# Attention and MoE on one core: the first four heads' scores in float32 from k and q as loaded, the row maxima of heads 1 and 2 tied by data to the preceding head's row, and fewer constant matmuls

## The chip, the cores and the metric

The program runs on one core of one Trainium2 chip. The metric is the device time of one execution in microseconds (us). Three executions of the kernel before took 1249.19, 1252.88 and 1254.61 us, a median of 1252.88 us.

## The reference

Two stages. The first is attention over 8 batches and 8 heads (64 heads in all) of 576 positions and 64 features, with a mask by blocks of 64 positions; the second is a gated feed-forward layer over all 4,608 rows.

```python
scores = scale * np.matmul(q, k.transpose(0, 1, 3, 2))
scores = np.where(block_i >= block_j, scores, -1000000000.0)
scores = scores - np.max(scores, axis=-1, keepdims=True)
attn = np.exp(scores)
attn = attn / (np.sum(attn, axis=-1, keepdims=True) + 1e-09)
x = np.matmul(attn, v)          # then heads side by side: 4608 x 512
h = x @ w_in                    # 512 -> 2048
out = (h * erf(softplus(h))) @ w_out   # 2048 -> 512
```

The inputs are float32 and the weights are float64 (the kernel loads them as pairs of 32-bit words and turns them into pairs of float16).

## The kernel before, in words

Heads are numbered n = 0 to 63. Each head's transposed k and q lie in a buffer `qk` of 128 partitions and four planes of 576 columns, in one of four such buffers that the heads use in turn (NB = 4). Planes 2 and 3, on partitions 0 to 63, hold k and q rounded to float32r (a float32 format that TensorE takes with reduced precision); under them, on partitions 64 to 68, stand five constant rows that bring in the mask and one row that is filled later, the negated row maximum of each query. Planes 0 and 1, on all 128 partitions, hold rounded values and remainders crossed, so that one product of 128 rows gives both first-order correction terms.

`load_qk` (line 380) fills a buffer. Its step `a` issues one DMA on GpSimd's queue (POOL) of three planes, which rounds on the way (L383), one on SyncE's queue (SP) of the plain float32 values into a staging tile `st` (L384), of which there are two, and a second rounding DMA of two planes on POOL (L385). Its step `c` forms the remainders with two subtractions on POOL (L388, L389).

`maxes` (line 396) computes the scores of a head once in float32r (L400, tiles `s`), takes row maxima on VectorE (L403, tile `mx`), transposes the five columns of maxima with a matmul against the identity (L430, tile `mt`), copies the result on ScalarE (L432) and sends it with a small DMA on ScalarE's queue into the row left free (L433). `probs` (line 440) computes the scores a second time, now transposed and with mask and maximum as extra rows, as two float32r matmuls that add up in one PSUM bank: 69 rows of rounded values (L446) and 128 rows of corrections (L447), tiles `t`; ScalarE's exponential follows (L451). `pv` multiplies by v (L495) and by ones for the sums (L518), for two heads at a time; for the first 24 heads these operands are plain float32. `normalise` turns this into rows of x, which go to DRAM in float16 pairs.

The loop over n (line 650) merges in each iteration: the loads of head n+3, the maxima of head n+2, the `mt` step of head n+1 in the iteration's first 60 per cent, the probabilities of head n, for even n the products with v of heads n-2 and n-1, a conversion or two of weights (`raw` tiles, loaded on SP, L113; converted by L120 to L126), and steps of the feed-forward layer (L190 upwards, L199 downwards) as soon as a batch of x is there. Before the loop the maxima of heads 0 and 1 are issued. In iterations 0 and 1, WARM = 10 matmuls of ones (L647) are merged in, whose result nobody reads. The order on each engine is that of a scheduler that goes by data dependences and its own costs; each engine then works through its own list in order.

## Time and profile before

| | before |
|---|---|
| median of three runs (range) | 1252.88 us (1249.19 to 1254.61) |
| the profiled execution | 1253.77 us, of which the span from first to last instruction is 1252.0 us |
| TensorE matmul (PE) busy | 1169.7 us, 93% of the span |
| ScalarE (ACT), VectorE (DVE), GpSimd (POOL) busy | 865.4, 791.9 and 515.9 us |
| DMA | 151.73 MB, 121 GB/s on average |
| mean granted TensorE clock | 0.97 of full speed |

The granted clock is given as a share of full speed; 1.00 is 2.4 GHz and 0.50 is 1.2 GHz, and a number between is a stretch with parts at either. An engine's busy share is an average over the program's stages, so the stages are read apart. In the rows below, "idle before" and its releaser stand in square brackets. SPq and ACTq are the queues on which SyncE and ScalarE issue DMAs; a long time there may include a wait for a buffer.

### The profile page before, as it was taken

What the parts mean: (1) busy time and instruction counts of PE and PEld (TensorE: products, weight loads), DVE (VectorE), ACT (ScalarE), POOL (GpSimd) and SP (SyncE); (2) the same over time, 40 slices, a digit from 0 to 9 for tenths busy, and PEclk for the clock granted to TensorE, in tenths of its full rate; (3) what the DMA queues carried; (4) which work ended last, traced back from release to release, by engine and by line L of the source; (5) the groups of instructions that cost most, each with busy time, mean ns of one, the idle gap of its engine ahead of it and who ended that gap; (6) DMA issues with size and microseconds to landing.
All of it is one profiled execution on the core that took longest, in us unless ns stands there. A gap on an engine that the chain in (4) does not pass through costs nothing.

```text
span 1252.0 us, 23446 instructions
## 1 busy us (share of the span) xinstructions
PE 1169.7 (93%) x9018; PEld 811.0 (65%) x9018; DVE 791.9 (63%) x1457; ACT 865.4 (69%) x1699; POOL 515.9 (41%) x486
## 2 busy tenths in 40 slices
PE   5788699989999999999999899999999999999896
PEld 2465466666666767767767677766777766666563
DVE  4677689787577666676657667666666644343433
ACT  1465577687676777877777677777777876666664
POOL 6455446545343444445444353545443313121211
PEclk9876799999999999999999999999999999999999
DMA  9988569744544455364454455455554121121211
GB/s 218 250 208 190 124 181 234 195 101 117 112 128 110 115 125 128 100 147 120 99 124 116 118 119 130 112 124 128 112 137 108 45 78 53 60 76 35 64 55 51
DMA packets 95741, 151.73 MB, mean 121 GB/s; under 512 B 7738, under 2 KB 44922, under 8 KB 95630
## 3 DMA queue, kind: packets, MB, share of 16 engines
q1 hardware_dynamic: 69840, 93.34, 25.7%
q0 software_dynamic: 25120, 56.66, 22.6%
q8 instruction: 71, 1.16, 0.4%
q10 hardware_dynamic: 670, 0.23, 0.2%
q14 instruction: 40, 0.33, 0.1%
HBM read 121.66 MB, written 28.31 MB: 120 GB/s over the span
## 4 chain that ended last, share of the span: by engine, by line
PE 49%; DVE 20%; ACT 18%; DMA 7%; issue 4%; POOL 1%; DVEq 0%; SPq 0%; POOLq 0%; ACTq 0%
PE m_h L190 16%; PE o L199 15%; PE u L495 5%; DVE m_r L163 4%; DVE m_r L164 4%; DVE m_r L165 3%; ACT m_r L160 3%; ACT m_r L162 3%; ACT m_r L161 3%; ACT m_r L159 3%; PE t L446 3%; PE s L400 3%; PE t L447 2%; DMA qk<-qk 2%; DMA qk<-mt 2%
## 5 line engine op out<-in xcount | busy, mean ns | idle before, releaser
L190 PE MATMUL m_h<-xh,w 128*128 128x256 f16 x2304 | 476.1, 276 | 19.5 <-DVE m_r L165 12.2
L190 PEld LDWEIGHTS <-w 128*128 128x128 f16 x3456 | 328.3, 99 | 158.1 <-issue 31.2
L199 PE MATMUL o<-w,m_gh 128*128 128x512 f16 x1152 | 334.1, 382 | 12.2 <-DVE pt L240 4.9
L167 POOL TENSOR_TENSOR m_gl<-m_r,m_gh 128x512 f16<-128x512 f32 x144 | 171.8, 1193 | 391.1 <-ACT m_gh L166 340.6
L190 PE MATMUL m_h<-xl,w 128*128 128x256 f16 x1152 | 316.8, 275 | 0.5 <-DMA xl<-x_d 0.5
L403 DVE TENSOR_REDUCE mx<-s 64x1 f32<-64x288 f32 (+4 forms) x384 | 174.5, 469 | 131.3 <-PE s L400 130.5
L163 DVE SCALAR_TENSOR_TENSOR m_r<-m_r,m_r 128x512 f32<-128x512 f32 x144 | 112.8, 783 | 197.3 <-ACT m_r L162 190.8
L199 PE MATMUL o<-w,m_gl 128*128 128x512 f16 x576 | 203.7, 384 | 0.3 <-POOL m_gl L167 0.3
L451 ACT ACTIVATE p<-t 128x288 f32<-128x288 f32 (+4 forms) x384 | 144.6, 384 | 79.4 <-PE t L447 69.1
L166 ACT CAST m_gh<-m_r 128x512 f16<-128x512 f32 x144 | 88.9, 617 | 157.2 <-DVE m_r L165 154.4
L446 PE MATMUL t<-qk 69*128 69x288 f32 (+4 forms) x384 | 168.2, 439 | 13.0 <-DMA qk<-mt 6.8
L400 PE MATMUL s<-qk 68*64 68x288 f32 (+3 forms) x384 | 150.1, 423 | 22.8 <-DMA qk<-qk 19.8
L159 ACT ACTIVATE m_r<-m_h,c,bs 128x512 f32<-128x512 f32 (+3 forms) x192 | 124.1, 666 | 44.5 <-PE m_h L190 41.4
L388 POOL TENSOR_TENSOR qk<-st,qk 64x576 fp32r<-64x576 f32 x64 | 95.9, 1499 | 127.2 <-DMA qk<-qk 124.5
L199 PEld LDWEIGHTS <-m_gh 128*128 128x128 f16 x1152 | 100.2, 98 | 67.6 <-issue 12.3
L164 DVE SCALAR_TENSOR_TENSOR m_r<-m_r 128x512 f32<-128x512 f32 x144 | 122.6, 852 | 3.3
L447 PE MATMUL t<-qk 128*128 128x288 f32 (+4 forms) x384 | 120.0, 313 | 0.0
L463 DVE TENSOR_TENSOR p<-p,p 128x832 f16<-128x832 f32 x80 | 81.7, 1022 | 58.0 <-ACT p L462 57.9
L389 POOL TENSOR_TENSOR qk<-st,qk 64x576 fp32r<-64x576 f32 x64 | 98.4, 1538 | 39.2 <-DMA qk<-qk 29.1
L161 ACT ACTIVATE m_r<-m_r,c 128x512 f32<-128x512 f32 x144 | 103.8, 721 | 2.7 <-ACT m_r L160 0.7
L162 ACT ACTIVATE m_r<-m_r,c 128x512 f32<-128x512 f32 x144 | 103.7, 720 | 2.3 <-ACT m_r L161 0.3
L160 ACT ACTIVATE m_r<-m_r,c 128x512 f32<-128x512 f32 x144 | 103.7, 720 | 1.6
(99 smaller groups left out, 1454.8 us busy)
## 6 DMA issues: line engine op xcount, KB each, us to landing
qk<-qk POOLq DMA_DIRECT2D x64, 432.0 KB, 5.0
st<-qk SPq DMA_DIRECT2D x64, 288.0 KB
qk<-qk POOLq DMA_DIRECT2D x64, 288.0 KB, 5.6
raw<-w SPq DMA_DIRECT2D x32, 512.0 KB
v<-v SPq DMA_DIRECT2D x16, 640.0 KB
x_d<-xs POOLq DMA_DIRECT2D x32, 288.0 KB, 3.3
xh<-x_d SPq DMA_DIRECT2D x36, 256.0 KB
xl<-x_d SPq DMA_DIRECT2D x36, 256.0 KB
```

Of the source, the lines that this page charges most:

```text
L159: nc.scalar.activation(r0s[:, :, lo:hi], h[:, :, lo:hi], AF.Tanh, bias=const(p1), scale=bss[b][g][:, 0:1])
L161: nc.scalar.activation(r0, r1, AF.Square, bias=const(b2), scale=a2)
L163: nc.vector.scalar_tensor_tensor(out=r0, in0=r0, scalar=c4, in1=r1, op0=ALU.add, op1=ALU.mult)
L164: nc.vector.scalar_tensor_tensor(out=r0, in0=r0, scalar=c5, in1=r0, op0=ALU.add, op1=ALU.mult)
L167: nc.gpsimd.tensor_tensor(out=gl, in0=r0, in1=gh, op=ALU.subtract)
L190: nc.tensor.matmul(h[:, k, :], lhsT=wf[:, a, sl], rhs=x[:, cc, :], start=cc == 0 and i == 0, stop=cc == NCC - 1 and i == 2)
L199: nc.tensor.matmul(o[c], lhsT=a[:, sl], rhs=wf[:, b_, :], start=u == u0 and k == 0 and not lo and b_ == 2, stop=u == u1 - 1 and k == nu - ...
L400: nc.tensor.matmul(dst[:r, :w_], lhsT=qh[:K, i * P : i * P + r], rhs=kh[:K, k0 : k0 + w_], start=True, stop=True)
L403: nc.vector.tensor_reduce(out=mx[:r, col : col + 1], in_=src, axis=AX.X, op=ALU.max, negate=True)
L446: nc.tensor.matmul(s[:kk, :w_], lhsT=kh[:K, ks], rhs=qh[:K, q0 : q0 + w_], start=True, stop=False)
L447: nc.tensor.matmul(s[:kk, :w_], lhsT=klh[:, ks], rhs=qhl[:, q0 : q0 + w_], start=False, stop=True)
L451: nc.scalar.activation(p32s[part][:kk, c : c + w_ - skip], s[:kk, skip:w_], AF.Exp, scale=SCALE)
```

## The change

For n < 4 (N32) `load_qk` issues two DMAs only: one on POOL that rounds k and q into the two planes of a new tile `ql` (for the maxima), and one on SP that brings them unrounded into a float32 tile `q32`. No staging tile, no remainders. `probs` of these heads issues one matmul of 69 rows in plain float32 instead of two in float32r. From head 4 on the old scheme stands, with the planes shared out over two tiles: `ql` has the two crossed planes and `qk` (taken in turn with `q32` out of one pool of four) the rounded k and q. Their loads are three DMAs on POOL (rounded k and q first, then one plane, then two) instead of two, with the same bytes, and for heads 4 to 7 a fourth of the constant rows. In `maxes` of heads 1 and 2, a transpose of the preceding head's maxima is written into each new bank before the scores overwrite it, so that these scores cannot be put ahead of the preceding head's maxima. WARM goes from 10 to 5 in each of the two iterations.

```diff
-    qks = [wpool.tile([P, 4 * S + 64], F32R, name=f"qk{i}", bufs=1) for i in range(NB)]
+    lows = [wpool.tile([P, 2 * S], F32R, name=f"ql{i}", bufs=1) for i in range(NB)]
+    qks = [wpool.tile([P, 2 * S + 64], F32, tag="qk", name=f"q32_{i}", bufs=NB) for i in range(NB)]
...
-            return qks[n % NB][:, i * S : (i + 1) * S]
+            return (lows if i < 2 else qks)[n % NB][:, i % 2 * S : (i % 2 + 1) * S]
...
-            t = qks[n % NB][:, : 4 * S].rearrange("p (i n) -> p i n", n=S)
+            if N32 <= n < N32 + NB:
+                qks[n % NB] = wpool.tile([P, 2 * S + 64], F32R, tag="qk", name=f"qk{n}", bufs=NB)
+            lo, hi = [x[n % NB][:, : 2 * S].rearrange("p (i n) -> p i n", n=S) for x in (lows, qks)]
+            if n < N32:
+                src = qk[b, h, : 2 * D].rearrange("(s d) n -> d s n", d=D)
+
+                def whole():
+                    nc.gpsimd.dma_start(lo[:D], src)
+                    nc.sync.dma_start(hi[:D], src)
+
+                return whole, lambda: None
...
-                nc.gpsimd.dma_start(t[:D, 1:4, :], qk[b, h, D:].rearrange("(s d) n -> d s n", d=D))
+                if n < N32 + NB:
+                    nc.gpsimd.dma_start(qks[n % NB][D : D + 5, : 2 * S], maskrows)
+                nc.gpsimd.dma_start(hi[:D], qk[b, h, : 2 * D].rearrange("(s d) n -> d s n", d=D))
+                nc.gpsimd.dma_start(lo[:D, 1, :], qk[b, h, D : 2 * D])
                 nc.sync.dma_start(st, qk[b, h, : 2 * D])
-                nc.gpsimd.dma_start(t[D:, 0:2, :], qk[b, h, : 2 * D].rearrange("(s d) n -> d s n", d=D))
+                nc.gpsimd.dma_start(lo[D:], qk[b, h, : 2 * D].rearrange("(s d) n -> d s n", d=D))
...
+            def bank(name):
+                s = anybank(name)
+                if n in (1, 2):
+                    nc.tensor.transpose(out=s[:5, :P], in_=mxs[(n - 1) % 2][:, :5], identity=ident)
+                return s
+            kh, qh = [part(n, i) for i in ((0, 1) if n < N32 else (2, 3))]
...
-                nc.tensor.matmul(s[:kk, :w_], lhsT=kh[:K, ks], rhs=qh[:K, q0 : q0 + w_], start=True, stop=False)
-                nc.tensor.matmul(s[:kk, :w_], lhsT=klh[:, ks], rhs=qhl[:, q0 : q0 + w_], start=False, stop=True)
+                nc.tensor.matmul(s[:kk, :w_], lhsT=kh[:K, ks], rhs=qh[:K, q0 : q0 + w_], start=True, stop=n < N32)
+                if n >= N32:
+                    nc.tensor.matmul(s[:kk, :w_], lhsT=klh[:, ks], rhs=qhl[:, q0 : q0 + w_], start=False, stop=True)
...
-        masks = [qks[n][D : D + 5, 2 * S : 4 * S] for n in range(NB)]
-        nc.gpsimd.dma_start(masks[0], maskrows)
-        for m in masks[1:]:
-            nc.scalar.dma_start(f32(m), f32(masks[0]))
+        nc.gpsimd.dma_start(lows[0][D : D + 4], maskrows[:4])
+        for n in range(NB):
+            if n:
+                nc.scalar.dma_start(f32(lows[n][D : D + 4]), f32(lows[0][D : D + 4]))
+            nc.scalar.dma_start(qks[n][D : D + 5, : 2 * S], maskrows)
...
-        WARM = 10
+        WARM = 5
```

The change also moves instructions. TensorE's list behind the maxima of head 0, before (the digit behind s01, s2, s3 and mt is the head; the last number of a name is the buffer's):

```order
L400 MATMUL s01_2_263<-qk2_130 128x256
L430 MATMUL mt0_223<-ident_77,mx0_146 5x128
L400 MATMUL s01_1_231<-qk1_129 128x256 x2
L400 MATMUL s2_1_236<-qk1_129 128x384
L400 MATMUL s3_1_239<-qk1_129 128x512
L400 MATMUL s01_2_263<-qk2_130 128x256
```

The same place of the changed kernel:

```order
L423 MATMUL s4_0_1_212<-ql0_128 64x288
L453 MATMUL mt0_219<-ident_77,mx0_150 5x128
L417 MATMUL s01_1_227<-ident_77,mx0_150 5x128
L423 MATMUL s01_1_227<-ql1_129 128x256 x2
L417 MATMUL s2_1_233<-ident_77,mx0_150 5x128
L423 MATMUL s2_1_233<-ql1_129 128x384
```

Head 0's `mt` stood behind a score of head 2; now it stands right behind head 0's own scores, and the ties (L417) stand ahead of head 1's.

SP's list from its third DMA on, before (`st_n` staging of head n, `v` and `raw` the first values of v and of the weights):

```order
L384 DMA st_1_165<-qk 128x576
L384 DMA st_2_166<-qk 128x576
L384 DMA st_3_252<-qk 128x576
L326 DMA v0_0_219<-v 128x1280
L113 DMA raw0_0_228<-w 128x1024
L113 DMA raw0_1_248<-w 128x1024
```

And of the changed kernel:

```order
L391 DMA q32_1_133<-qk 64x2x576
L391 DMA q32_2_134<-qk 64x2x576
L391 DMA q32_3_135<-qk 64x2x576
L401 DMA st_4_320<-qk 128x576
L401 DMA st_5_388<-qk 128x576
L330 DMA v0_0_215<-v 128x1280
L114 DMA raw0_0_224<-w 128x1024
```

The staging loads of heads 4 and 5 now stand ahead of v and of the first weights, and four loads go to four tiles of their own, where three had to share two.

POOL's list at the loads of heads 4 to 6, before:

```order
L383 DMA qk0_128<-qk 64x3x576
L385 DMA qk0_128<-qk 64x2x576
L383 DMA qk1_129<-qk 64x3x576
L388 TENSOR_TENSOR qk0_128<-st_4_328,qk0_128 64x576
L389 TENSOR_TENSOR qk0_128<-st_4_328,qk0_128 64x576
L385 DMA qk1_129<-qk 64x2x576
L388 TENSOR_TENSOR qk1_129<-st_5_404,qk1_129 64x576
L389 TENSOR_TENSOR qk1_129<-st_5_404,qk1_129 64x576
L383 DMA qk2_130<-qk 64x3x576
```

And of the changed kernel (L398 constant rows, L399 rounded k and q, L400 and L402 the crossed planes, L405 and L406 the subtractions):

```order
L398 DMA qk4_319<-maskrows 5x1152
L399 DMA qk4_319<-qk 64x2x576
L402 DMA ql2_130<-qk 64x2x576
L398 DMA qk5_387<-maskrows 5x1152
L405 TENSOR_TENSOR ql0_128<-st_4_320,qk4_319 64x576
L399 DMA qk5_387<-qk 64x2x576
L400 DMA ql3_131<-qk 64x576
L402 DMA ql3_131<-qk 64x2x576
L405 TENSOR_TENSOR ql1_129<-st_5_388,qk5_387 64x576
L406 TENSOR_TENSOR ql2_130<-st_6_508,ql2_130 64x576
L398 DMA qk6_507<-maskrows 5x1152
L399 DMA qk6_507<-qk 64x2x576
```

The main load of head 5 (L399) now stands behind a subtraction of head 4, which needs head 4's main load, and that of head 6 behind a subtraction of head 6 itself, which needs its staging load; before, L383 of either stood ahead of its own head's subtractions. From the first feed-forward matmuls on, the lists of TensorE, ScalarE and VectorE agree row for row but for a few places, with the new names.

## Rows read from the trace of the kernel before

**Rows 1.** The head of the page: the span of the profiled execution.

```profile
span 1252.0 us, 23446 instructions
```

**Rows 2.** Busy time of the engines in stretches: the first 160 us, all that follows, and two microseconds of the first stage. Behind the stretch stand its length, then busy us and instructions of PE, PEld, DVE, ACT and POOL, the granted clock, the DMA engines' share (over 1 where packets overlap) and GB/s.

```profile
0.00:160.00 160.00, 119.74 (x705) 77.97 (x706) 103.84 (x235) 79.75 (x198) 81.17 (x95) 0.81 0.87 200
160.00:1252.00 1092.00, 1049.95 (x8316) 732.99 (x8313) 688.10 (x1223) 785.67 (x1501) 434.77 (x392) 0.99 0.43 110
28.00:30.00 2.00, 1.12 (x5) 0.33 (x5) 2.00 (x7) 1.52 (x4) 1.58 (x2) 1.00 0.21 81
```

**Rows 3.** What PE waited for in the first 160 us: us in total, times, the longest.

```profile
PE s L400 <- DMA qk<-qk: 19.8, 6, 9.3
...
PE t L446 <- DMA qk<-mt: 6.8, 5, 2.9
```

**Rows 4.** The chain of waits through the first 60 us, in order of time: start, length, what.

```profile
3.90 10.50 DMA qk<-qk
14.47 1.41 POOL qk L389
...
16.84 8.15 DMA raw<-w
...
26.44 3.44 DMA qk<-mt
...
31.44 7.53 DMA qk<-mt
...
52.06 4.92 DMA qk<-mt
```

**Rows 5.** Timeline of SP's queue: start, length (with a wait for a buffer), what.

```profile
1.64 14.58 SPq L384 DMA_DIRECT2D st<-qk  x3
16.27 0.47 SPq L326 DMA_DIRECT2D v<-v  x1
16.84 4.05 SPq L113 DMA_DIRECT2D raw<-w  x2
...
49.16 0.33 SPq L384 DMA_DIRECT2D st<-qk  x1
```

**Rows 6.** Timeline of VectorE where head 0's maxima end.

```profile
12.53 0.13 DVE L325 COPY v<-mx 1x1 f32<-1x1 f32 x1
```

**Rows 7.** DMA in the first 30 us: total; the two queues that matter (POOL's is q0, SP's is in q1) with packets, MB and the time of their packets as a share of 16 engines' 30 us; POOL's issues of three and of two planes with the median time to landing.

```profile
DMA packets 2930, 6.75 MB, mean 225 GB/s; under 512 B 468, under 2 KB 478, under 8 KB 2930
...
q0 software_dynamic: 1440, 2.97, 62.4%
q1 hardware_dynamic: 1440, 3.71, 40.2%
...
qk<-qk POOLq DMA_DIRECT2D x5, 432.0 KB, 7.1
...
qk<-qk POOLq DMA_DIRECT2D x4, 288.0 KB, 9.1
```

**Rows 8.** Timeline of PE: the first and the last probability scores of heads 0 and 1 in this order, and the first of head 2; idle time before and its releaser in brackets.

```profile
24.75 0.40 PE L446 MATMUL t<-qk 69*128 69x288 f32 x1
...
32.61 0.31 PE L447 MATMUL t<-qk 128*128 128x320 f32 x1
...
39.01 0.61 PE L446 MATMUL t<-qk 69*128 69x288 f32 x1 [2.94 <-DMA qk<-mt]
```

**Rows 9.** Timeline of PE, prices: two scores of 288 columns in float32r, the products with v of two heads in float32 (twice), and the sums with ones. Starts count, since matmuls overlap.

```profile
50.76 0.29 PE L446 MATMUL t<-qk 69*128 69x288 f32 x1
50.89 0.30 PE L447 MATMUL t<-qk 128*128 128x288 f32 x1
...
40.27 4.87 PE L495 MATMUL u<-p,v 128*64 128x256 f32 x28
...
57.94 4.56 PE L495 MATMUL u<-p,v 128*64 128x256 f32 x28
...
64.19 1.74 PE L518 MATMUL us<-p,ones 128*32 128x384 f32 x32
```

**Rows 10.** Busy time in the stretches of those five; the columns are those of rows 2, the granted clock the third number from the end.

```profile
50.50:53.30 2.80, 2.80 (x19) 2.33 (x17) 2.80 (x11) 1.93 (x8) 1.24 (x2) 1.00 0.96 330
...
40.30:45.10 4.80, 4.80 (x30) 2.63 (x29) 3.02 (x4) 2.53 (x7) 2.25 (x3) 0.62 1.23 277
...
57.90:62.50 4.60, 4.60 (x30) 2.56 (x29) 1.72 (x3) 2.12 (x6) 2.59 (x3) 0.66 1.24 272
...
64.20:65.90 1.70, 1.70 (x34) 1.19 (x33) 1.70 (x6) 1.70 (x6) 0.50 (x1) 1.00 0.40 136
```

**Rows 11.** POOL's groups over the whole span: busy us and mean ns, idle time before and releasers.

```profile
L167 POOL TENSOR_TENSOR m_gl<-m_r,m_gh 128x512 f16<-128x512 f32 x144 | 171.8, 1193 | 391.1 <-ACT m_gh L166 340.6 <-ACT p L451 25.1 <-issue 20.8
...
L383 POOL DMA_DIRECT2D qk<-qk x64 | 41.4, 646 | 129.0 <-PE t L447 112.1 <-PE o L199 12.6 <-PE s L400 3.7
L385 POOL DMA_DIRECT2D qk<-qk x64 | 39.8, 622 | 0.0
```

**Rows 12.** What PE waited for after 160 us, the row that names POOL.

```profile
PE o L199 <- POOL m_gl L167: 0.3, 1, 0.3
```

**Rows 13.** Timeline of PE, two places where it waited for a later head's load.

```profile
55.74 0.50 PE L400 MATMUL s<-qk 68*128 68x256 f32 x2 [2.35 <-DMA qk<-qk]
...
74.47 0.79 PE L400 MATMUL s<-qk 68*128 68x256 f32 x2 [1.39 <-DMA qk<-qk]
```

More of the change, by code (lines that the diff above doesn't have):

```diff
@@ L49, in tile_attention_moe @@
     B32 = 3
+    N32 = 4
     SH = 384
@@ L307, in tile_attention_moe, with anybank @@
         turn = []
-        def bank(name):
+        def anybank(name):
             turn.append(0)
@@ L317, in bank @@
             return ps_a.tile([P, 512], F32, tag="a", name=name)
+        bank = anybank
         def load_v(b, qd, src):
@@ L373, in part @@
         def part(n, i):
[L375 removed]
+            return (lows if i < 2 else qks)[n % NB][:, i % 2 * S : (i % 2 + 1) * S]
         def load_qk(n):
             b, h = divmod(n, H)
[L379 removed]
+            if N32 <= n < N32 + NB:
[7 more added lines that the diff above has]
+                return whole, lambda: None
             st = apool.tile([P, S], F32, tag="st", name=f"st_{n}", bufs=2)
             def a():
[L383 removed]
+                if n < N32 + NB:
+                    nc.gpsimd.dma_start(qks[n % NB][D : D + 5, : 2 * S], maskrows)
+                nc.gpsimd.dma_start(hi[:D], qk[b, h, : 2 * D].rearrange("(s d) n -> d s n", d=D))
+                nc.gpsimd.dma_start(lo[:D, 1, :], qk[b, h, D : 2 * D])
                 nc.sync.dma_start(st, qk[b, h, : 2 * D])
[L385 removed]
+                nc.gpsimd.dma_start(lo[D:], qk[b, h, : 2 * D].rearrange("(s d) n -> d s n", d=D))
             def c():
[L388 to L389 removed]
+                nc.gpsimd.tensor_tensor(out=lo[:D, 0, :], in0=st[:D, :], in1=f32(hi[:D, 0, :]), op=ALU.subtract)
+                nc.gpsimd.tensor_tensor(out=lo[D:, 1, :], in0=st[D:, :], in1=f32(lo[D:, 1, :]), op=ALU.subtract)
             return a, c
@@ L395, in maxes @@
             mx, K = mxs[n % 2], D + 4
-            kh, qh = part(n, 2), part(n, 3)
+            def bank(name):
[4 more added lines that the diff above has]
+            kh, qh = [part(n, i) for i in ((0, 1) if n < N32 else (2, 3))]
             def mm(dst, i, k0, w_):
@@ L428, in e @@
                 nc.vector.tensor_reduce(out=mx[:64, 4:5], in_=mx[:64, 5:7], axis=AX.X, op=ALU.min)
-                pt = bank(f"mt{n}")
+                pt = anybank(f"mt{n}")
                 nc.tensor.transpose(out=pt[:5, :P], in_=mx[:, :5], identity=ident)
```

4 lines of the change are left out of this document (1 added, 3 removed).

## The prediction

> **What bounds the kernel now.** I read the busy time by stretches first, then PE's waits and the chain of waits in the early stretch, then the timelines of SP and PE, then the DMA queues. After 160 us PE is busy 1,050 of 1,092 us at a clock of 0.99 [rows 2]; there only PE work counts, and the lists say that from the first feed-forward matmuls on nothing is reordered. So the change is worth what it does to the first 160 us, where PE is idle 160 - 119.7 = 40.3 us, at a clock of 0.81 [rows 2]. PE's waits there name loads of k and q (19.8 us) and the small transfers of the maxima (6.8 us) [rows 3]. The chain shows how: 10.5 us of loads, a POOL subtraction, the weights' first load (8.15 us), then one transfer of maxima after the other, 3.44, 7.53 and 4.92 us [rows 4]. A transfer of 2.5 KB takes that long because it shares the DMA engines with the loads. The reader is to see a start that hangs on DMA: whatever comes earlier at head 2 or 4 moves everything behind it, because the later stretch has no slack to swallow a shift.
>
> **The first loads.** Per head of the first four, 432 + 288 KB on POOL and 288 KB on SP become 288 KB on each. What goes is 432 KB four times, 1.77 MB. POOL's queue held 16 engines for 62.4% of 30 us for 2.97 MB, 6.3 us per MB; SP's 40.2% for 3.71 MB, 3.25 us per MB [rows 7]. So up to 1.77 x 6.3 = 11.1 us of engine time goes, or 11.1/1.13 = 9.8 us of time, since the queues' shares add up to 1.06 over 30 us, of which the first two hold nothing. That is the ceiling; the floor is nothing, if the stage were all latency (at 28 to 30 us the engines were indeed busy for 0.21 only [rows 2]).
>
> The Trainium skill ("DMA: Bandwidth & Descriptors", "Issuing engines are not separate DMA queues") says that DMAs of all issuing engines run on the same 16 engines and interleave. By it only the bytes count, and 1.77 MB at the mean of 225 GB/s would be an estimated 7.9 us; the two prices per MB above speak for more [rows 7].
>
> Where between floor and ceiling, I work out along the chain. SP's third staging load waited for a buffer that the subtraction ending at 14.47 + 1.41 us freed; so v and weights were issued at 16.27 and 16.84 only [rows 4, 5]. In the changed list nothing ahead of them waits for POOL. What remains is VectorE's copy behind head 0's maxima, at 12.53 us [rows 6], and head 0's load shrinks from 432 to 288 KB, a third of 7.1 us [rows 7]: 12.5 - 2.4 = 10.1, so the weights go out at 10.8, 6.0 us earlier. Two staging loads stand ahead of them now, 590 KB at 3.25 us per MB = 1.9 us. So 4.1 to 6.0 us; I take 5.0. ScalarE's first exponential stands behind that load (25.0 us in the chain), and head 0's scores at 24.75 [rows 8] come with it. The new place of head 0's `mt` is needed for this and, by itself, worth nothing more.
>
> Then the hand-off to head 2, 7.53 us [rows 4]. It shared the engines with 432 + 288 + 288 KB of head 4, 432 KB of head 5, v and two weights; now the staging loads and crossed planes of heads 4 and 5 can be past, and a third of the bytes is gone. From 0 to 4.1 us (it would then be as short as the 3.44); I take a third, 2.5 us.
>
> **The float32 scores.** Not in the trace for this shape. A float32r score of 288 columns starts 0.13 us after the one before, 0.47 ns per column; two per score are 0.94 [rows 9]. Float32 products with 32-row outputs, four side by side, take 1.74 us for the 3,200 columns of a pair of heads at full clock, 0.54 ns per column, so 2.2 if one has the array to itself; those with 64 rows, two side by side, 4.56 us at a clock of 0.66, 1.43 ns per column, or 2.85 alone, 1.9 at full clock [rows 9, 10]. I take 2.0. Bounds: 0.54 (nothing side by side is lost) and 2.85.
>
> The Trainium skill ("FP8 and Floating Point Precision", "TensorE Precision Notes") speaks against the change here: true float32 takes four passes. Four times 0.47 is 1.9, and the sum's cost below would be 3.7 instead of 4.1 us; the products' rows, at 1.9 to 2.2 alone, agree with it [rows 9].
>
> A head has 1,856 columns. What of the extra 2.0 - 0.94 = 1.06 ns lies on the path: of head 0 the three pieces ahead of head 1's `mt` (832 columns), of heads 1 and 3 the two ahead of the next `mt` (576 each; the rest falls in PE's waits for the transfer), of head 2 all, because iteration 2 keeps PE busy. 3,840 columns x 1.06 = 4.1 us; at the bounds -1.5 and +7.3.
>
> **The clock.** Head 2's scores begin after a wait of 2.94 us in a stretch with hardly any PE work since 32.6 us [rows 8], and the products behind them ran at 0.62, 4.87 us [rows 9, 10]. Those of full clock would take 3,200 x 2.0/2 = 3.2 us. With a longer head 1 and an earlier head 2 the idle stretch shrinks from 6 to about 2 us; I take 2.0 us of gain for products and scores together (bounds 0 and 3).
>
> **The rest.** Heads 4 on: k and q come as 288 KB ahead of the others instead of within 432; PE waited 2.35 and 1.39 us for such loads [rows 13], and the loads take 7.1 us [rows 7]. A third less would end both; but the constant rows ahead and the subtractions now in front of heads 5 and 6 take part of it back. I take 1.5 us (bounds -7.5, second rival, and 3.7). The ties are ten short matmuls, two or three on the path ahead of head 2's scores: 0.3 us (bounds 0 and 1.3, ten starts of 0.13 us [rows 9]; the wait for the preceding maxima adds nothing where the next head's load lands later than these end, 12.5 us [rows 6]). Ten constant matmuls fewer: nothing, since the first exponential waited for the weights, not for them; if that load came early, they would no longer be in the way. One more POOL issue per head, 60 x 0.63 = 38 us [rows 11]: nothing, since POOL waits 391 us for ScalarE before its feed-forward subtractions, and PE waited for these 0.3 us in all [rows 11, 12]. If that cover were gone, it would be at most those 38 us.
>
> **The sum.** 5.0 + 2.5 + 2.0 + 1.5 - 4.1 - 0.3 = 6.6 us off the profiled execution's 1253.8 (its span of 1252.0 [rows 1] and 1.8 around it): 1247.2. That execution lay 0.9 above the median of the runs, so 1246.3, say 1246 us, 0.5% faster.
>
> **The rivals.**
> - Nothing that counts. The weights' load keeps its place behind the two staging loads and gains 2 us only; the hand-off to head 2 is latency; float32 costs its upper bound: 2 + 1 + 1 + 1 - 4.5 = 0.5 us, 1252. For it: the engines were idle at 28 to 30 us [rows 2], so not all is bandwidth. Against it: 10.5 and 8.15 us of loads in the chain [rows 4].
> - Slower. POOL's list holds head 6's main load behind a subtraction that needs head 6's staging load, which SP issues behind weights; before, that staging load went out at 49.16 [rows 5] and its data were used only after PE had its scores. If it goes out no earlier now, it lands 7.1 us later (as the other loads [rows 7], 56.3), the subtraction of 1.4 us ends at 57.7, the constant rows and the main load follow, 1.3 us to issue [rows 11] and two thirds of 7.1 to land, 63.7 instead of the 55.7 at which PE began head 6 [rows 13]: 8 us late, less for heads 7 and 8, about 12 in sum against a gain of 6: 1259. It decides from where that staging load is issued later than some 8 us ahead of the end of head 2's scores. Against it: its buffer is free after head 4's first subtraction, which by the steps above (head 0's scores done near 23, 1.3 us to issue head 4's load, 4.7 to land, 1.4 to subtract) is near 31 us, so SP should issue it near 35.
> - Larger gain. The stage is bandwidth throughout and the ceiling of 9.8 us comes in full, the clock's 3 and the loads' 3: 9.8 + 3 + 3 - 2.5 = 13 us, 1240.
> - The change does what it says (the lists show it), so a fourth is not needed.
>
> **How the numbers follow.** The forecast's own range is 1241 to 1250, chance 0.60, of which 0.42 lies below 1246.6, that is faster by over 0.5% (6.3 us, about what a measurement of this kernel can tell). Nothing that counts: 0.19. Slower: 0.12, of which 0.10 lies above 1259.1 and the rest within 0.5%. Larger gain: 0.09. So faster 0.51, same 0.39, slower 0.10. The range of 8 in 10 takes in the larger gain's better half and the first rival: 1238 to 1254.
>
> **What would show it.** Weights issued on SP by 11 to 13 us and landed near 20; head 0's scores on PE near 20 instead of 24.75; head 2's first score near 31 to 32 instead of 39.0; its products with v at a clock near 1; the first feed-forward matmul 6 to 7 us earlier than before; the stretch after it as long as before. Float32 scores of 288 columns should start 0.5 to 0.6 us apart at full clock. Wrong would be: head 2 earlier but the first feed-forward matmul not (then something between them bounds), head 6's load landing later than 50 us, or a difference that arises after the first 160 us.

## The result, and the profile after

Twenty executions of the changed kernel took 1257.64 us in the median (1250.78 to 1267.68), twenty of the kernel before on the same chip 1249.24 us (1241.49 to 1258.41): a ratio of 1.0070 with an interval of 1.0049 to 1.0091. (A ratio here is worked out from all executions of a batch and differs a little from the quotient of the two medians.) The change makes the kernel 0.7% slower. The prediction was 1246 us, 0.5% below the 1252.88 of three executions and 0.3% below the 1249.24 of twenty, and its range ended at 1254. One execution of all those below (1281.17 us, the traced one of e15) ran in a slower state and is left out of e15's ratio and of what is read from traces.

Two traces of the changed kernel are read side by side in the following, since they differ in the first stage: the one taken with the result (1255.88 us) and one of the same program run again (experiment e9_after_again, 1259.26 us). Two of the kernel before stand against them: the one of the rows ahead of the prediction, and e1_before_again (1248.48 us). First the span and the busy time of the first 160 us and of the rest, of the changed kernel, columns as in [rows 2]:

```profile
span 1254.1 us, 23598 instructions
...
0.00:160.00 160.00, 127.80 (x755) 81.68 (x755) 114.79 (x243) 85.31 (x209) 76.62 (x100) 0.84 0.79 193
160.00:1254.00 1094.00, 1044.64 (x8266) 729.63 (x8264) 685.60 (x1215) 782.19 (x1490) 455.69 (x438) 0.99 0.42 109
```

The same of its second trace:

```profile
span 1257.5 us, 23598 instructions
...
0.00:160.00 160.00, 132.79 (x706) 84.42 (x707) 109.54 (x236) 80.68 (x197) 74.41 (x99) 0.86 0.78 190
```

PE's idle time in the first 160 us fell, as the prediction wanted: 40.3 us before [rows 2], 32.2 and 27.2 us now. That is the same as saying that its busy time rose, from 119.7 to 127.8 and 132.8 us, and in the second trace the stage is no further at 160 us than before: the first feed-forward product comes at 142.8 us, where it came at 140.3. What is less idle is not earlier.

PE's waits over the first 160 us, us in total, times, the longest, against [rows 3]:

```profile
PE s L423 <- DMA ql<-qk: 8.8, 1, 8.8
PE s L423 <- DMA qk<-qk: 5.0, 2, 3.1
PE mt L453 <- DVE mx L451: 4.3, 2, 2.7
PE t L469 <- DMA q<-mt: 2.6, 2, 2.4
PE t L469 <- DMA qk<-mt: 2.4, 2, 1.7
PE s L423 <- DMA ql<-ql: 1.8, 1, 1.8
```

The waits for loads of k and q are down from 19.8 to 8.8 + 5.0 = 13.8 us (10.5 in the second trace, 21.0 in e1_before_again). The row of maxima is waited for 2.6 + 2.4 = 5.0 instead of 6.8 us; since e1_before_again has 2.4, that is no gain. Two waits are new, and no step of the prediction has them: the transposed maxima wait for VectorE, and head 1's scores wait 1.8 us for a copy of the constant rows into `ql`.

The start of SP's queue, against [rows 5]:

```profile
5.57 1.36 SPq L401 DMA_DIRECT2D st<-qk  x2
12.19 0.33 SPq L330 DMA_DIRECT2D v<-v  x1
14.72 9.09 SPq L114 DMA_DIRECT2D raw<-w  x3
```

Then PE in the first 62 us: head 0's first probability score, that of head 2, head 4's scores, and the products with v of two pairs of heads, against [rows 8, 9, 13]:

```profile
21.52 1.83 PE L469 MATMUL t<-q 69*128 69x288 f32 x4
...
27.67 1.21 PE L469 MATMUL t<-q 69*128 69x288 f32 x4
28.50 0.56 PE L423 MATMUL s<-ql 68*128 68x384 f32 x1
...
35.52 0.75 PE L469 MATMUL t<-q 69*128 69x288 f32 x2 [2.38 <-DMA q<-mt]
...
39.39 0.76 PE L423 MATMUL s<-qk 68*128 68x256 f32 x2 [3.12 <-DMA qk<-qk]
...
41.04 4.14 PE L519 MATMUL u<-p,v 128*64 128x256 f32 x28
...
57.63 3.07 PE L519 MATMUL u<-p,v 128*64 128x256 f32 x28
```

The first score is 3.2 us earlier than before and head 2's is 3.5 us earlier, but head 4's scores are later than before, and the first products come later too (41.04 instead of 40.27 us). Head 4's scores before, and its main load on POOL's queue:

```profile
35.60 0.47 PE L400 MATMUL s<-qk 68*128 68x256 f32 x2 [2.67 <-DMA qk<-qk]
...
29.76 0.64 POOL L383 DMA_DIRECT2D qk<-qk  x1
```

In the second trace of the changed kernel, head 0's and head 1's first probability scores with the score that follows the latter, and the products:

```profile
22.72 2.26 PE L469 MATMUL t<-q 69*128 69x288 f32 x4 [1.27 <-DMA q<-mt]
...
32.93 2.29 PE L469 MATMUL t<-q 69*128 69x288 f32 x4
34.61 0.94 PE L423 MATMUL s<-ql 68*128 68x384 f32 x1
...
45.45 5.38 PE L519 MATMUL u<-p,v 128*64 128x256 f32 x28
...
63.31 2.81 PE L519 MATMUL u<-p,v 128*64 128x256 f32 x24
```

Why head 4 is late stands on POOL's list:

```profile
26.13 1.43 POOL L406 TENSOR_TENSOR ql<-st,ql 64x576 fp32r<-64x576 f32 x1 [6.80 <-issue]
27.51 0.62 POOL L402 DMA_DIRECT2D ql<-qk  x1
32.95 1.39 POOL L406 TENSOR_TENSOR ql<-st,ql 64x576 fp32r<-64x576 f32 x1 [4.83 <-DMA ql<-qk]
34.30 0.55 POOL L400 DMA_DIRECT2D ql<-qk  x1
34.84 0.54 POOL L398 DMA_DIRECT2D qk<-maskrows  x1
35.37 0.64 POOL L399 DMA_DIRECT2D qk<-qk  x1
```

Head 4's main load (L399) goes out at 35.37 us; before it went out at 29.76. Ahead of it POOL waits for crossed planes of heads 4 and 5 and subtracts.

To see where the time comes from, I count the feed-forward products into `m_h` (3,456 in every trace; the first has number 0 in the count) and take the time from one to another, in us:

| stretch | before | e1_before_again | after | e9_after_again |
|---|---|---|---|---|
| start to the 1st product | 140.3 | 139.4 | 136.1 | 142.8 |
| 1st to 240th | 117.3 | 115.6 | 117.1 | 119.3 |
| 240th to 288th | 13.9 | 13.5 | 16.6 | 15.7 |
| 288th to 1600th | 439.4 | 435.6 | 435.0 | 433.1 |
| 1600th to 2400th | 261.4 | 262.9 | 266.3 | 264.0 |
| 2400th to the last | 261.7 | 261.7 | 262.4 | 262.0 |
| last to the end | 18.0 | 18.0 | 20.6 | 20.6 |

The means differ by -0.4, +1.7, +2.5, -3.5, +2.9, +0.5 and +2.7 us, 6.4 in sum, which is what the means of the spans differ by. Four more traces differ from these in ties or constant matmuls alone (e12 and e13 from the changed kernel, e14 and e18 from the kernel before, all below). Four against four it is -1.0, +3.4, +2.3, -1.9, +3.0, +0.3 and +2.5 us, 8.6 in sum. So the first stage gives next to nothing, and the loss sits in three places: from the 1st to the 288th product, from the 1600th to the 2400th, and at the end.

### The profile page after: what moved, and what is told of

It reads as the page before. It is cut to its first block, busy times and chain, and to the rows that moved or that the text cites. A ratio compares the mean times of both kernels' runs of the same rounds, so it can differ in the third digit from the quotient of the medians.

```text
span 1254.1 us, 23598 instructions
## 1 busy us (share of the span) xinstructions
PE 1172.4 (93%) x9018; PEld 811.3 (65%) x9018; DVE 800.4 (64%) x1457; ACT 867.5 (69%) x1699; POOL 532.3 (42%) x538
## 4 chain that ended last, share of the span: by engine, by line
PE 45%; DVE 23%; ACT 19%; DMA 7%; issue 4%; POOL 1%; DVEq 0%; ACTq 0%; POOLq 0%; SPq 0%
PE m_h L191 15%; PE o L200 14%; DVE m_r L165 5%; DVE m_r L164 5%; PE u L519 4%; DVE m_r L166 4%; ACT m_r L161 3%; ACT m_r L162 3%; ACT m_r L163 3%; PE t L469 3%; ACT m_r L160 3%; PE s L423 3%; DVE mx L426 2%; PE t L471 2%; DMA v<-v 2%
## 5 line engine op out<-in xcount | busy, mean ns | idle before, releaser
L469 PE MATMUL t<-qk 69*128 69x288 f32 (+1 forms) x360 | 160.6, 447 | 11.9 <-DVE mx L426 6.9
L423 PE MATMUL s<-qk 68*128 68x256 f32 (+1 forms) x360 | 143.8, 427 | 7.5 <-DMA qk<-qk 5.0
L406 POOL TENSOR_TENSOR ql<-st,ql 64x576 fp32r<-64x576 f32 x60 | 91.4, 1523 | 76.6 <-DMA ql<-qk 62.8
L487 DVE TENSOR_TENSOR p<-p,p 128x832 f16<-128x832 f32 x80 | 85.1, 1063 | 55.4 <-ACT p L486 55.2
L405 POOL TENSOR_TENSOR ql<-st,qk 64x576 fp32r<-64x576 f32 x60 | 91.1, 1519 | 68.5 <-DMA qk<-qk 68.1
L471 PE MATMUL t<-ql 128*128 128x288 f32 (+1 forms) x360 | 113.3, 315 | 0.0
```

The costliest lines, as they stand in the source:

```text
L423: nc.tensor.matmul(dst[:r, :w_], lhsT=qh[:K, i * P : i * P + r], rhs=kh[:K, k0 : k0 + w_], start=True, stop=True)
L469: nc.tensor.matmul(s[:kk, :w_], lhsT=kh[:K, ks], rhs=qh[:K, q0 : q0 + w_], start=True, stop=n < N32)
```

## The experiments

Every kernel here has its order on each engine from the scheduler anew. The traces show that order: only in e5, e6 and e10 (and in the repeats e1 and e9) do PE, VectorE and ScalarE work through the same rows in the same order as in the kernel that was edited. Every other edit also moved rows of these three engines, up to some 90 to 100 us in e4, e14 and e18, to 160 to 230 us in e3, e12, e13, e15 and e16, to 260 us in e8 and to 300 to 315 us in e2, e7, e11 and e17.

**Groups of edits alone (e1 to e4).** e1 is the kernel before again. e2 splits its three-plane load:

```diff
-                nc.gpsimd.dma_start(t[:D, 1:4, :], qk[b, h, D:].rearrange("(s d) n -> d s n", d=D))
+                nc.gpsimd.dma_start(t[:D, 2:4, :], qk[b, h, : 2 * D].rearrange("(s d) n -> d s n", d=D))
+                nc.gpsimd.dma_start(t[:D, 1, :], qk[b, h, D : 2 * D])
```

e3 gives the kernel before the float32 scores of heads 0 to 3, with k and q unrounded in slots that the weights fill later, and leaves all else as it was; e4 adds the ties and WARM = 5.

```diff
+                if n < N32:
+                    nc.tensor.matmul(s[:kk, :w_], lhsT=plain(n, 0)[:K, ks], rhs=plain(n, 1)[:K, q0 : q0 + w_], start=True, stop=True)
```

> The kernel before, unchanged, as a control. Every theory expects a ratio to the kernel before of 1.000 within about 0.3%, and a last drain on POOL of about 8 us. What it is for: how far one execution of the same program lies from another, and how far that goes with the mean granted clock; if the spread of 8 us either way that the runs show comes from the clock of the first 160 us, the runs' times fall with their granted clock by about 6 us for each 0.005.

> The kernel before with one part of the change alone: from head 0 on, the first POOL load of a head (three planes) is issued as two (k and q, then one plane), the same bytes, 64 more loads. Theory A, that the third load per head is what costs: POOL's last drain, 7.97 us before and 10.17 after, grows by 37 ns for each load, so to about 10.3 us, and the loop loses the rest, in sum 5 to 9 us slower, 1.004 to 1.007. Theory B, that the first four heads' part costs: only the drain, 2.3 us, about 1.002. Theory C, that only the early clock differs: 1.000 but for the drain.

> The kernel before with float32 scores of heads 0 to 3 alone: k and q of these heads go unrounded, by SP, into two weight tiles that are not in use yet, and rounded by one POOL load into the old buffers for the maxima; from head 4 on the old two loads, no ties, 10 constant matmuls. Theory A: no loss, and as the early bytes go and POOL has no subtractions of heads 0 to 3, 3 to 7 us faster than before, 0.994 to 0.998, head 4's load on POOL at once behind head 0's scores. Theory B: 4 to 8 us slower, 1.003 to 1.006, like the change.

> The same as the run before it with the ties of heads 1 and 2 and 5 instead of 10 constant matmuls per iteration: the whole change but for the third load per head and the two-tile layout. Theory A: faster than before by 3 to 8 us, 0.993 to 0.998. Theory B: slower by 6 us, 1.005, and slower than the run without ties and with 10 constant matmuls by what these two cost. A last drain of about 8 us under both.

| | median, us | ratio to before | interval |
|---|---|---|---|
| e1_before_again | 1248.79 | 0.9992 | 0.9972 to 1.0013 |
| e2_split_loads | 1259.54 | 1.0084 | 1.0049 to 1.0119 |
| e3_float32_old_loads | 1250.11 | 1.0010 | 0.9984 to 1.0036 |
| e4_float32_ties_warm | 1252.88 | 1.0026 | 1.0003 to 1.0050 |

The third load, with the new order that comes with it, costs as much as the whole change. The float32 part, which was to gain, gains nothing in either form. Its traces (e3, e4 and e16 below) have the clock up for 3.4 us near 22 to 28 us and then at the lower level for 24 to 34 us, so most of these float32 scores ran at the lower level.

**Where the third load costs (e5, e6, e7, e17).** The split of e2, for some heads only: 48 and 57 (e5), 24 to 63 but those two (e6), 0 to 23 (e7), 4 to 23 (e17). In e5 and e6 the lists of PE, VectorE and ScalarE are those of the kernel before, row for row; in e7 and e17 they are not.

```diff
+                if n in (48, 57):
...
+                else:
+                    nc.gpsimd.dma_start(t[:D, 1:4, :], qk[b, h, D:].rearrange("(s d) n -> d s n", d=D))
```

The two heads were chosen because of this: in the changed kernel and in e2, and not in the kernel before, VectorE's subtraction into `p` took 2.3 and 3.2 us there. The second place in the changed kernel, POOL, VectorE and PE:

```profile
862.90 0.74 POOL L604 DMA_DIRECT2D x_d<-xs  x1
863.29 3.20 DVE L487 TENSOR_TENSOR p<-p,p 128x768 f16<-128x768 f32 x1
863.64 0.61 POOL L402 DMA_DIRECT2D ql<-qk  x1
864.25 1.42 POOL L405 TENSOR_TENSOR ql<-st,qk 64x576 fp32r<-64x576 f32 x1
...
866.54 1.10 PE L519 MATMUL u<-p,v 128*64 128x128 f16 x20 [2.26 <-DVE p L487]
```

And in e1_before_again:

```profile
861.05 0.74 POOL L580 DMA_DIRECT2D x_d<-xs  x1
...
861.80 0.95 DVE L463 TENSOR_TENSOR p<-p,p 128x768 f16<-128x768 f32 x1
...
863.21 1.41 POOL L388 TENSOR_TENSOR qk<-st,qk 64x576 fp32r<-64x576 f32 x1 [1.42 <-DMA qk<-qk]
```

Before, VectorE is through in 0.95 us before POOL's subtraction begins. With a third load POOL's work has moved: VectorE's operation ends 0.82 us behind the end of POOL's subtraction (864.25 + 1.42 = 865.67), that is, it hardly advanced beside it, and PE waits 2.26 us. It had also hardly advanced in the 0.96 us ahead of that, in which POOL issued two DMAs; no row says why.

Whether a collision comes is a matter of time, not of the list alone. In the second trace of the changed kernel the one at head 57 is there again (866.9 us, 3.20 us), the one at head 48 is not, and one at head 35 has come (483.4 us, 2.18 us). In e13, which has the changed kernel's third loads, no subtraction into `p` takes over 2.0 us, as in the kernel before.

> The kernel before, with the three-plane load split in two for heads 48 and 57 alone. Collision theory (the third load costs where a POOL subtraction that it moves falls onto a VectorE operation on the path): most of what heads 24 to 63 lose is lost at these two, the subtraction into p takes 2.3 and 3.2 us there instead of 0.96, and the time is 3 to 5 us above the kernel before, about 1252 to 1253. Issue theory (every third issue costs the same, 10.8 us over 64 heads): 0.3 us.

> The same split for heads 24 to 63, except 48 and 57. Collision theory: no VectorE subtraction over 2.1 us, no cost in the loop, at most 2 us either way from POOL's last drain: ratio 0.998 to 1.002. Issue theory: 38 of 64 heads, 6.4 us, ratio 1.005.

> The same split for heads 0 to 23. Collision theory: about 6 us (what the split of all heads cost, 10.8, less the 4.5 of heads 48 and 57), part of it in the first loads; issue theory: 24 of 64 heads, 4.1 us. The trace is to show whether the loss comes before the first feed-forward product (3 us there in the split of all heads) or near 190 and 255 us.

> The kernel before with the three-plane load split in two for heads 4 to 23 alone, the heads below 24 that have a third load in the changed kernel. If the third load costs there as it did in heads 0 to 23 (ratio 1.0109), the changed kernel's loss is that of the third load: ratio 1.006 to 1.011, and the stretch between the 240th and 288th feed-forward product takes 15.5 to 16.5 us instead of 14. If the cost was that of the first four heads' loads, which the changed kernel doesn't have: 0.998 to 1.003.

| | median, us | ratio to before | interval |
|---|---|---|---|
| e5_split_two_heads | 1251.82 | 1.0025 | 0.9993 to 1.0057 |
| e6_split_late_but_two | 1248.80 | 0.9999 | 0.9967 to 1.0031 |
| e7_split_early | 1261.89 | 1.0109 | 1.0071 to 1.0148 |
| e17_split_4_to_23 | 1255.83 | 1.0058 | 1.0029 to 1.0086 |

The issue theory falls: 38 late heads with a third load cost nothing (it wanted 6.4 us; the interval ends at 0.31%, 3.9 us). One collision there is in e6 too, near 545 us (3.26 us for the subtraction), and shorter stretches elsewhere outweigh it. The early heads carry the cost, and those that the changed kernel also has, 4 to 23, lose 0.58% alone, 1247.35 x 0.0058 = 7.2 us. In e17's trace the 288th product comes at 277.7 us, 7.7 us behind the mean of the two traces of before.

But e17 is not the third load alone. Its split moves VectorE's rows up to 309 us, and the order that comes of it is that of e2, e7 and, from 151 us on, of the changed kernel. After a weight step (`w`) VectorE did one step of `m_r` and the next weight steps, in e1_before_again:

```profile
258.49 0.74 DVE L147 SCALAR_TENSOR_TENSOR w<-w,wsb,w 128x512 f16<-128x512 f32 x1
259.15 0.68 DVE L165 SCALAR_TENSOR_TENSOR m_r<-m_r,m_h 128x512 f32<-128x512 f32 x1
259.75 2.56 DVE L147 SCALAR_TENSOR_TENSOR w<-w,wsb,w 128x512 f16<-128x512 f32 x2
262.23 1.36 DVE L529 SCALAR_TENSOR_TENSOR bs<-bi,wsb 128x1 f32<-128x1 f32 x1
```

In the changed kernel two other steps of `m_r` stand between two weight steps, and the second runs beside a POOL subtraction (265.68 to 267.15 us), 1.79 us instead of 0.69:

```profile
264.53 0.75 DVE L148 SCALAR_TENSOR_TENSOR w<-w,wsb,w 128x512 f16<-128x512 f32 x1
265.19 0.68 DVE L164 SCALAR_TENSOR_TENSOR m_r<-m_r,m_r 128x512 f32<-128x512 f32 x1
265.91 1.79 DVE L165 SCALAR_TENSOR_TENSOR m_r<-m_r 128x512 f32<-128x512 f32 x1
267.62 0.74 DVE L148 SCALAR_TENSOR_TENSOR w<-w,wsb,w 128x512 f16<-128x512 f32 x1
```

The stretch from the 240th to the 288th product takes 15.3 to 16.6 us in all eight traces with this order there (after, e2, e7, e9, e10, e12, e13, e17), and 13.3 to 14.5 us in the eleven others. In each of the eight a VectorE step 11.8 to 12.8 us into it takes 1.8 to 1.9 us beside a POOL subtraction, in none of the eleven. So the 2.3 us lost in this stretch go with the new order and with that collision. Whether e17's 7.2 us come of the third load on POOL's queue or of the new order of the other engines, no run separates.

The two heads are inconclusive as a time, 3.1 us with an interval that takes in zero, but the trace shows the price of one collision. From the 2000th to the 2400th feed-forward product eight traces in which a subtraction of that stretch took over 2.6 us need 131.7 to 133.5 us (the changed kernel, e2, e5, e8 to e12), eleven without need 129.7 to 131.4. In e5, which splits nothing else there and has the collision at head 57 but none at head 48, it is 132.6.

**Mending it in the changed kernel (e8, e10, e11).** e8 issues the one-plane load behind the subtractions. e10 brings this plane, from head 24 on, with a plain copy on SP's queue; there only the lists of POOL and SP differ from the changed kernel's. e11 does so from head 4 on.

```diff
-                nc.gpsimd.dma_start(lo[:D, 1, :], qk[b, h, D : 2 * D])
+                if n < 24:
+                    nc.gpsimd.dma_start(lo[:D, 1, :], qk[b, h, D : 2 * D])
...
+                if n >= 24:
+                    nc.sync.dma_start(f32(lo[:D, 1, :]), f32(hi[:D, 1, :]))
```

> The changed kernel, with the one-plane load (lo[:D, 1]) issued behind the two subtractions instead of ahead of them. Collision theory: two loads stand ahead of the subtractions again, so the two stretched VectorE subtractions near 704 and 863 us go and the time falls by 4 to 5 us, to 1252 to 1253, unless the subtractions fall onto others. Issue theory: as many issues as in the changed kernel, so its time, 1257 to 1258.

> The changed kernel once more, for a second trace beside the first. 1256 to 1259 us. If the account is right, the first feed-forward product comes at 136 to 137 us (139 to 140 in the kernel before), the subtractions into p that take 2.2 and 3.2 us stand at the same heads (48 and 57), and POOL's last drain takes 10.2 us again (8.0 before).

> The changed kernel, where from head 24 on the one-plane load on POOL is replaced by a plain copy of the rounded plane on SP's queue: POOL issues two loads per head again, and no list but POOL's and SP's changes. Collision theory: the two stretched subtractions go, 4 to 5 us, and with POOL's drain, if it goes by the loads, 2 us more: 1251 to 1254. Rival (the loss has no place in the late heads, since the split there cost nothing in the kernel before): 1256 to 1259.

> The same from head 4 on, so that POOL has two loads per head everywhere. If the third load also costs in heads 4 to 23, as the split of the early heads suggests (14.8 us in the kernel before), it is faster than with the copy from head 24 on, by 2 to 6 us: 1246 to 1252; if SP's copies, which wait for the rounded planes, hold up the weights behind them, it is slower than that one and the first feed-forward product comes later than 137 us.

| | median, us | ratio to before | interval |
|---|---|---|---|
| e8_after_plane_last | 1259.35 | 1.0095 | 1.0063 to 1.0128 |
| e9_after_again | 1257.83 | 1.0079 | 1.0052 to 1.0105 |
| e10_after_sp_from_24 | 1257.77 | 1.0077 | 1.0050 to 1.0103 |
| e11_after_sp_from_4 | 1269.74 | 1.0159 | 1.0120 to 1.0198 |

None mends it. e10 shows that two loads instead of three are not the point in the late heads; VectorE, POOL and PE of e10:

```profile
796.95 2.84 DVE L490 TENSOR_TENSOR p<-p,p 128x768 f16<-128x768 f32 x1 [0.63 <-ACT p L489]
797.54 1.42 POOL L408 TENSOR_TENSOR ql<-st,qk 64x576 fp32r<-64x576 f32 x1
...
799.84 1.44 PE L522 MATMUL u<-p,v 128*64 128x128 f16 x19 [1.43 <-DVE p L490]
```

The collision at head 48 is gone, that at head 57 has stayed (near 870 us, 2.66 us), and one at head 53 has come, here near 797 us. e8 has those of heads 48 and 57, near 708 and 869 us, and two more, near 547 and 796; the other engines' lists moved in it too, up to 260 us. A change of POOL's loads reshuffles which VectorE operation its subtractions meet. e11, with two loads per head on POOL throughout, is the slowest of the three; with SP's copies waiting on its queue, in a list that was reordered too, nothing was learned of the early third load in the changed kernel.

**The ties and the constant matmuls (e12 to e16, e18).** e12 takes the ties out of the changed kernel; e13 gives it WARM = 10; e14 and e18 are the kernel before with WARM = 5; e15 is e10 with WARM = 10; e16 is e4 with WARM = 10.

```diff
-        WARM = 10
+        WARM = 5
```

The second trace of the changed kernel led to them. There a transpose of 128 columns still took 0.41 us at 28.61 us; in the first trace it took 0.28 at 23.19, and in e1_before_again 0.27 at 25.45. Over 20 to 50 us the granted clock is 0.89 in the first trace and in both of the kernel before; for the second trace none is recorded before 50 us, but by these durations TensorE was at the lower of its two levels, and its float32 scores took twice as long (below).

> The changed kernel without the ties of heads 1 and 2 (a score of head 2 stands ahead of head 0's row of maxima again, as before). By the prediction's steps the row's earlier place costs nothing where head 2's load is there early: the same time within 2 us, first feed-forward product at 136 to 138. Rival: the ties are what the early gain comes from; then head 0's scores come near 24 instead of 21.5 us, and that product at 139 to 140.

> The changed kernel with WARM = 10 as before. Clock theory (with half the constant matmuls TensorE's clock falls, or does not rise, in the first 50 us, and the gain of the first loads is lost in float32 scores at half clock): the granted clock is up from about 22 us to past 45 us but for short stretches, the third group of products with v comes near 57.6 us as in the first trace of the changed kernel and not at 62 to 63 as in its repeats, and the time falls by 3 to 5 us: 1252 to 1255. Rival (as predicted, these matmuls are worth nothing): 1257 to 1258.

> The kernel before with WARM = 5 and nothing else. Clock theory: the clock rises later or falls earlier in the first 50 us than in the kernel before, where it rose at 22 to 24 us in each of four traces; 2 to 5 us slower, 1249 to 1252. Rival: 1247, as before.

> The changed kernel with WARM = 10, and from head 24 on the one-plane load as a copy on SP's queue. It should take both: the early clock (3 to 5 us), and the shorter end that the copy on SP's queue showed (17.5 instead of 20.6 us from the last feed-forward product to the end): 1250 to 1253. If neither adds up: 1257.

> The kernel before with float32 scores of the first four heads in the old loads and the ties, WARM = 10: between the run without ties (WARM = 10, ratio 1.0010) and the run with ties and WARM = 5 (1.0026). If the constant matmuls were what cost there, 1.000 to 1.001 and the first feed-forward product near 134; if the ties were, 1.0026 and near 145.

> The kernel before with WARM = 5 once more. If the gain of that part alone is real: ratio 0.993 to 0.998, first feed-forward product at 135 to 136 us. If it was a chance of that batch: 0.999 to 1.001 and 139 to 140 us.

| | median, us | ratio to before | interval |
|---|---|---|---|
| e12_after_no_ties | 1256.54 | 1.0071 | 1.0044 to 1.0097 |
| e13_after_warm10 | 1260.29 | 1.0077 | 1.0053 to 1.0101 |
| e14_before_warm5 | 1242.44 | 0.9948 | 0.9921 to 0.9976 |
| e15_after_warm10_sp_from_24 | 1266.50 | 1.0122 | 1.0080 to 1.0164 |
| e16_float32_ties | 1256.24 | 1.0053 | 1.0026 to 1.0079 |
| e18_before_warm5_again | 1245.05 | 0.9990 | 0.9963 to 1.0017 |

The clock theory is right on the clock and wrong on the time. In the seven traces with the kernel before's first loads and WARM = 10 (before, e1, e2, e5, e6, e7, e17) the granted clock rises at 20.9 to 24.5 us; with WARM = 5 the first rise is recorded at 44.1 and 48.3 us (e14, e18). In the changed kernel WARM = 10 keeps it up from 22.6 to 46.5 us (e13), where the first trace had it up from 22.8 to 36.4 and the second not before 50.2. The time does not follow: more constant matmuls do not help the changed kernel, and fewer make the kernel before no slower, in one batch even 0.5% faster, though the repeat does not confirm it (first feed-forward product at 135.1 us in the one, at 139.1 in the other). The ties of the changed kernel are worth nothing. Without them its trace has head 0's first score at 25.61 us and the first feed-forward product at 135.4 all the same: that product does not hang on how early head 0 is. Nor is an early first product kept: where it came at 134.0 to 135.8 us (e3, e12, e13, e14), the way to the 240th took 120.6 to 129.4 us, in the four traces of the table 115.6 to 119.3. The two gains of e15 did not add up; there was none. In the old loads the ties came with a loss (e16 against e3: 1.0053 and 1.0010, intervals that just overlap). The kernel before with WARM = 5 has the lowest medians of all that was run, 1242.44 and 1245.05 us; that it beats the kernel before is shown by one batch of two.

## Why the prediction was wrong

**Every gain was placed in the first 160 us; the loss arose where it was said that nothing changes.** Two steps failed. The first is the premise "the lists say that from the first feed-forward matmuls on nothing is reordered". The lists agree row for row only from about 306 us on. Between the first feed-forward product and there some 84 of 251 rows of VectorE and 73 of 275 of ScalarE stand elsewhere than before, in the order that the split loads alone bring (e2, e7, e17), and from the 1st to the 288th product the loss is 3.4 + 2.3 = 5.7 us, four traces against four.

The second is "One more POOL issue per head ... nothing, since POOL waits 391 us". The rows under it were right: POOL still waits 392 us for ScalarE's results, and the 60 issues of one plane cost it 33 us that it has to spare. The issue itself costs nothing that could be measured where no other list changes (e6). But the cover was tested for the wrong thing. I asked whether PE waits for POOL's results [rows 11, 12]. What a moved load changes is when POOL's subtractions run, and beside them VectorE's operations can stand still, which are on the path. From the 1600th to the 2400th product that is shown: 266.3, 264.0, 266.9 and 261.8 us in the traces with two, one, two and no collisions more than before (after, e9, e12, e13), 260.0 to 262.9 in the four of before. In heads 4 to 23, where VectorE also converts weights, the third load and the order that it brings cost 7.2 us (e17); that collisions make up all of it is not shown. In the changed kernel the loss there shows as VectorE's rows that PE waits for. Over 160 to 1240 us:

```profile
PE t L469 <- DVE mx L426: 5.9, 5, 2.0
...
PE u L519 <- DVE p L487: 3.1, 2, 2.3
```

Before, the first of these rows had 2.0 us and the second did not exist; in e1_before_again 2.6 us and none. e17 has 6.0 us in the first and no second. How much of the 8.4 us the early third load takes in the changed kernel itself was not settled: the one kernel with the old loads and the rest of the change, e4, lost 0.26% where the change lost 0.70 and 0.79%, but e16, the same with more constant matmuls, lost 0.53%.

**The first loads (5.0 us)** gave 3.2 us at head 0's first score in one trace and 2.0 in the other. The term of the shorter load failed: head 0's first product came at 8.82 and 10.51 us, before at 9.32 and 7.62, so two planes were there no earlier than three, where 2.4 us were counted. The weights went out at 14.72, not 10.8: v ahead of them at 12.19, as the copy of 12.5 us would have it without the shorter load, and the weights 2.5 us behind v (0.7 in the second trace), for which no row names a reason. ScalarE began on them at 22.78 and 24.99 us, before at 25.01 and 23.92. Nor does head 0's score come with them: in the second trace it came 2.3 us ahead of ScalarE's start.

**The hand-off to head 2 (2.5 us).** From head 0's to head 2's first score it took 35.52 - 21.52 = 14.0 us, before 39.01 - 24.75 = 14.3 [rows 8] and in e1_before_again 37.66 - 24.63 = 13.0. With the float32 scores that lie between, there is no gain beyond what two traces of one program differ by.

**Heads 4 on (+1.5 us)** had the wrong sign: -3.8 us at head 4's scores (35.60 before, 39.39 after; 37.09 in e1_before_again). This is the mechanism of the rival that ended slower, a main load behind a subtraction on POOL's list, at head 4 instead of head 6, and what the subtraction waited for is a crossed plane's load, not the staging tile. At head 6 the rival's own wait came too: SP issued that staging load at 42.25 us, not 35, the subtraction at 49.91 waited 3.64 us for it, and the main load went out at 52.33. But PE began head 6 at 57.30, 1.6 us later than before and without a wait, where the rival had 8 us. By 57.6 us head 4's delay was made up in the first trace, so it is not the loss either.

**Float32 (4.1 us)** was cheaper at full clock than I took it. The trace has two records for each of these scores. In the row at 27.67 us the last three start 0.24 us apart, 0.49 us per score of 288 columns or 1.7 ns per column, where I took 2.0 between 0.54 and 2.85; 3,840 columns x (1.7 - 0.94) = 2.9 us. (The row behind, at 28.50, starts 0.03 us behind the last record, while that one is recorded until 28.88 us, so it does not tell the price.) What failed is the clock term beside it: I counted 2.0 us of gain for a shorter pause. In the second trace the same records of head 1 start 0.48 us apart, twice as far, and PE was busy 52.3 of the first 66 us, in the first 46.5, before 42.6. Longer products at the lower level eat the gain of the earlier start. Which level the changed kernel has in that stretch differs between executions of one program. The number of constant matmuls moves it (e13, e14, e18), but the time did not follow.

**The ties and constant matmuls** (0.3 us and nothing): nothing in the changed kernel, as said.

**The first rival** ("nothing that counts", 1252 us) charges float32 with 4.5 us and calls that its upper bound, which was worked out as 7.3 us. With 7.3 it would have ended 2.3 us slower than before, near 1255.

**The end.** From the last feed-forward product to the end it took 20.6 instead of 18.0 us, in both traces; no step spoke of it. The last stores go out 0.5 us earlier than before (1245.36 against 1245.90 us). The last long row is POOL's closing drain, which begins ahead of these stores: it starts at 1242.70 us and is recorded with 10.17 us in the changed kernel, at 1243.24 us and with 7.97 us in the kernel before. The end does not grow with the number of POOL's loads: the splits e2, e5, e7 and e17 end after 16.1 us. What sets it stays open.

## What to carry to other kernels

An engine with hundreds of idle microseconds is not free to take work, if it and the engine on the path hold each other up: ask what each of its operations runs beside, not only who waits for its result. A change of one small transfer per head moves all that is timed by it, so a steady stretch that one calls unchanged needs a price for being reshuffled, some 2 us for each operation on the path that is caught. Whether it is unchanged is to be counted, row by row and engine by engine; "but for a few places" hid a third of VectorE's rows for 170 us. The same count tells which experiment changes one thing alone. And where two executions of one program differ by 6.7 us at the first milestone, one trace cannot show a gain of 4.

## What the hardware showed that I had not expected

A VectorE operation with two inputs in on-chip memory can stand still while a POOL subtraction runs: 0.95 us alone, up to 3.2 us beside one. In the four traces of the table 81 to 90 VectorE operations, most of them steps of `m_r` and `w`, take over 0.3 us longer than the median of their kind, and every one overlaps a POOL subtraction. They cost VectorE 74 and 80 us before and 82 and 76 us in the changed kernel. So the change does not bring more of this; it moves it. Nor does an overlap always cost: of 24 subtractions into `p` of the changed kernel that overlapped a POOL subtraction, four took over 1.6 us; in the kernel before, of 26, two did. POOL's DMA issues alone do not lengthen them: the 19 beside these took 0.97 us in the mean, at most 1.03, the 37 that met nothing 1.00. The Trainium skill ("SBUF — State Buffer", "SBUF: two separate sides") states that VectorE and GpSimd share a pair of ports, and that an operation of VectorE with two inputs there and one of GpSimd that reads shut each other out for a whole instruction. The rows agree with that, at 2.26 us of PE's time for one case. They don't show its other half, that the one that starts first goes first: at 863.29 us VectorE's start is recorded ahead of POOL's subtraction, and it ended behind it.

The first stage of one and the same program varies: the changed kernel's first feed-forward product came at 136.1 and at 142.8 us, while in four traces of the kernel before or with the same lists up to there (before, e1, e5, e6) it came between 139.3 and 140.3.
